# Memory values with the weights held in the array, first tiles and weights reordered over two queues, early out-projection in half portions

## The chip, the cores and the metric

The kernel runs on one core of a Trainium2 chip. TensorE multiplies matrices into PSUM, VectorE (DVE) and ScalarE (ACT) copy and compute, GpSimd (POOL) does element-wise work in SBUF, and SyncE (SP) and ScalarE have queues on which transfers are issued to the core's 16 DMA engines. The metric is the device time of one execution in microseconds; the median of the runs is compared.

## The reference

Two independent computations share a call and their outputs are joined along the last axis.

```python
# part A: a diagonal complex state space model over L = 2048 tokens, 1024 states
Bu = jnp.einsum('bld,pd->blp', x + 0j, B_bar)
for t in range(L):
    h = Lam_bar[None, :] * h + Bu[:, t, :]
y = 2.0 * jnp.einsum('blp,dp->bld', hseq, Cmat).real + x * Dskip[None, None, :]
# part B: attention in segments of 32 tokens, with 8 memory rows carried over
for s in range(n_seg):                       # 64 segments, 32 heads of 128
    h = concat([mem, x[s]], axis=1)          # 8 + 32 rows
    q, k, v = h @ Wq, h @ Wk, h @ Wv
    p = softmax(mask(q @ k.T * scale))
    o = (p @ v) @ Wo
    mem, out_s = o[:, :8], o[:, 8:]
```

(The lines of part B are shortened.) Each segment's memory is an output of the segment before it, so part B is a recurrence over 64 steps.

## The kernel before

**Part B without the recurrence.** The kernel guesses all memories first. `og` and `guess` compute, from the means of the segments, a memory row for each segment; the rows together with the given memory stand in `memT`, which is the last 73 columns (`NM`) of `xe`. `xe` holds the tokens turned (feature on the partition, token along the row). Attention then runs over all segments at once, three to a group of 96 columns, and `check` compares the guesses with what attention gave; a flag decides whether a loop with the plain recurrence (`general`) runs afterwards. In the profile it doesn't run.

**Stages.** (1) From the start to 360 us: values of the tokens (V = x Wv, one block of 4 heads at a time, 8 blocks, `v_first` and `v_pair`) are interleaved with the first half of part A (`stage1`, `post`). (2) To about 465 us: `stage2` of part A with `guess` between. (3) From 465 to 1025 us: projections of Q and K (`proj`, 18 steps for each of 16 pairs of heads), attention (`attention`, 11 units for each pair), and the values of the memory rows (`v_mem`), all interleaved by the loop in `kernel_main`: after each attention unit as many projection steps run as the count `want` says. When all projection steps are done, at unit 165 of 176, each further unit takes one piece of `early`, a part of the out-projection whose operands are ready. (4) To the end: the rest of the out-projection (`op_some`, `op`, `evac`) with `check` between.

**The order of the work.** Instructions are written in program order; a scheduler places them on each engine and may move one that is ready ahead of others. `keep_in_program_order` puts an instruction behind the one written before it on its engine. In the timeline the engines follow the written order in the loop of stage 3, while loads are issued as soon as a buffer is free.

**Around the changed places.**

- The opening: `load_rows` (L369) brings 128 tokens as rows; `turn_rows` (L372) transposes them on TensorE, 8 pieces into one PSUM tile of tag "O", and one copy (VectorE for even tiles, ScalarE for odd ones) writes them into `xe`. `v_first` (L441) turns tiles 0 to 2, then multiplies with pieces of the first Wv block for three tiles at a time, turns tile 3 before the last pieces and ends with tile 3's matmuls. The loads stand at L875 to L881: tile 0, 2 and half of the Wv pieces on SyncE's queue, tile 1, 3 and the other half on ScalarE's. Six matmuls on a cleared piece of SBUF (L887 to L891) run while the first tile is on its way.
- Memory values: `v_mem` (L497) holds 73 columns of `memT` in the array and streams 512 columns of Wv through it, 8 times; the result has memory rows on the partitions, and ScalarE copies it to SBUF, from where 7 rows go to `vx` and 66 to `vt` in DRAM. `load_v` (L580) reads both back for each pair of heads. It is called once between projection steps 9 and 10 for block 0, and at unit 4 of head pairs 0 to 6 for blocks 1 to 7.
- Early out-projection: `op_some` (L672) yields after each `op`, which is 8 matmuls; (0,0) and (1,0) with three groups of heads make six pieces.
- PSUM: tags "P", "S" and "O" with two buffers each. Projections, `v_mem` and `early` use "P", attention scores "S", attention outputs "O". A matmul into a buffer waits until its former content has been copied out.

Of the kernel before, what the change touches and what calls it, by code (L numbers as in the profile page):

```python
# [9 lines left out]
BF16 = mybir.dt.bfloat16  # L10
# [16 lines left out]
HB = 8; HP = 16  # L27
# [7 lines left out]
NMX = 7  # L35
NM = NTL + NMX
# [280 lines left out]
class PartB:  # L317
    def __init__(self, k, x, mem0, Wq, Wk, Wv, Wo, out):
        self.k = k
        self.x, self.mem0, self.out = x, mem0, out  # L320
        self.Wf = [w.rearrange("(c p) h e -> p c (h e)", p=128) for w in (Wq, Wk, Wv)]
        self.Wo = Wo.rearrange("h e d -> e h d")
        self.vx = [k.drp.tile([NSLOT, 512], BF16, name=f"b_vx{i}") for i in range(HB)]
        self.vt = [k.drp.tile([NTL, 512], BF16, name=f"b_vt{i}") for i in range(HB)]
        self.os = [k.drp.tile([T, 1024], BF16, name=f"b_os{i}") for i in range(4)]
        self.omd = k.drp.tile([MT, H * E], BF16, name="b_omd")
        self.od = k.drp.tile([128, H * L], BF16, name="f_od")
        c = k.cst
        self.m0T = c.tile([128, KC, M], BF16, name="b_m0T")
        self.gm = c.tile([128, KC, NM], FP32, name="b_gm")  # L330
        self.xbar = c.tile([128, KC, NSEG], BF16, name="b_xbar")
        self.ogT = c.tile([128, H, NSEG], BF16, name="b_ogT")
        self.accE = c.tile([128, HP * NU], FP32, name="b_accE")
        self.rall = c.tile([128, HP * NU * 4], FP32, name="b_rall")
        self.flag = c.tile([1, 1], I32, name="b_flag")
# [30 lines left out]
            if lo < hi:  # L366
                k.SP.dma_start(self.xe[:, :, lo:hi], self.x[0][lo + r:hi + r, :], transpose=True)

    def load_rows(self, t, n, xr, e):  # L369
        e.dma_start(xr[:, t:t + n, :], self.x[0][t * 128 + 64:(t + n) * 128 + 64, :].rearrange("(i p) d -> p i d", p=128))  # L370

    def turn_rows(self, t, xr):  # L372

        k = self.k
        pt = k.ps("O", (128, 1024), BF16)
        for c in range(KC):
            k.tc.keep_in_program_order(k.PE.transpose(pt[:, c * 128:(c + 1) * 128], xr[:, t, c * 128:(c + 1) * 128], k.ident[:]))
        k.copy("vs"[t % 2], self.xe[:, :, t * 128:(t + 1) * 128], pt[:].rearrange("p (c n) -> p c n", c=KC))

    def sum_x(self, q, pool):  # L380

# [59 lines left out]
    def v_first(self, w, xr, e):  # L441

        k = self.k
        for t in range(3):
            self.turn_rows(t, xr)
        p = [k.ps("A") for t in range(4)]
        for j in range(4):
            for t in range(3):
                self.v_mm(p[t], t, w, range(2 * j, 2 * j + 2))
            if j == 2:  # L450
                self.turn_rows(3, xr)
        self.v_mm(p[3], 3, w, range(KC))
        for q in range(2):
            st = self.v_tile()
            for i in range(2):
                k.copy("s", st[:, i, :], p[2 * q + i][:])
                if i == 0:
                    yield
            self.v_st(0, q, st, e)
            yield  # L460
# [34 lines left out]


    def v_mem(self, hb):  # L497
        k = self.k
        w = self.load_wv(hb)
        p = k.ps("P")  # L500
        for c in range(KC):
            k.PE.matmul(p[0:NM, :], self.memT[:, c, :], w[:, c, :], start=(c == 0), stop=(c == KC - 1))
        st = self.p3.tile([NM, 512], BF16, name="b_vmst", bufs=2)
        k.copy("s", st[:], p[0:NM, :])
        k.SP.dma_start(self.vx[hb][64:64 + NMX, :], st[0:NMX, :])
        k.SP.dma_start(self.vt[hb][:], st[NMX:NM, :])


    def qk_init(self, pool):
        V, G = self.k.V, self.k.G  # L510
        self.qk = []
        for i in range(2):
            pair = []
            for n in "qk":
                t = pool.tile([128, 2, QW], BF16, name=f"b_{n}{i}", bufs=1)
                V.memset(t[:, :, 64 + NMX:GX], 0.0)
                V.memset(t[:, :, 21 * GW + 64:21 * GW + GX], 0.0)
                V.memset(t[:, :, NG * GW:QW], 0.0)
                pair.append(t)
            self.qk.append(pair)  # L520
        self.vb, self.mb = [], []
        for i in range(2):
            t = pool.tile([GW, NG, VW], BF16, name=f"b_v{i}", bufs=1)
            G.memset(t[:, :, 0:1], 1.0)
            G.memset(t[:, :, VW - 1:VW], 1.0)
            self.vb.append(t)
        for i in range(4):
            t = pool.tile([GW, 4 * GW + 32], BF16, name=f"b_m{i}", bufs=1)
            G.memset(t[:, 4 * GW:4 * GW + 32], 0.0)
            self.mb.append(t)  # L530
# [129 lines left out]
    def wo_half(self, half, h):  # L660
        return self.wo0[h // 8][:, h % 8, :] if half == 0 else self.wo1[:, h, :]

    def op(self, t, half, q):

        k = self.k
        ol = self.ol[t // 4, q]
        tt = t % 4
        for h8 in range(8):
            h = 8 * q + h8
            k.PE.matmul(self.acc[t, half], ol[:, h8, tt * 128:(tt + 1) * 128], self.wo_half(half, h), start=(h == 0), stop=(h == H - 1))  # L670

    def op_some(self, which, qs, tag):  # L672
        o = None
        for n, (t, half) in enumerate(which):
            if tag != "O":
                self.acc[t, half] = self.k.ps(tag)[:]
            else:
                if n % 2 == 0:
                    o = self.k.ps("O")
                self.acc[t, half] = o[:, n % 2, :]  # L680
            for q in qs:
                self.op(t, half, q)
                yield

    def evac(self, t, half):
        k = self.k
# [159 lines left out]
def kernel_main(tc, A_x, A_Lre, A_Lim, A_Bre, A_Bim, A_Cre, A_Cim, A_logdt, A_Dskip, B_x, B_mem0, B_Wq, B_Wk, B_Wv, B_Wo, out,  # L846
                force=False, dbg=None):
    with ExitStack() as ctx:
# [16 lines left out]
        with pool("p1", "right") as p1:  # L865
# [6 lines left out]
            a.tab = a.wp = a.btp = b.vst = p1  # L872
            a.jf = b.rall[:, 0:TB + 1]
            xr = tmp[:, 4096:8192].rearrange("p (t d) -> p t d", t=4)
            b.load_rows(0, 1, xr, k.SP)  # L875
            b.load_rows(1, 1, xr, nc.scalar)
            b.load_rows(2, 1, xr, k.SP)
            for j in range(4):
                b.load_wv(0, wvs[0], 4, (nc.scalar, k.SP)[j % 2], [j])
            b.load_rows(3, 1, xr, nc.scalar)  # L880
            b.load_wv(1, wvs[1], 2)  # L881
            a.load_params(tmp)
            k.SP.dma_start(tmp[0:M, 0:D], b.mem0[0])
            b.load_x(512, 1024)
            b.load_x(1024, 1536)
            b.load_x(1536, T)
            wu = tmp[:, 2048:2560]  # L887
            k.V.memset(wu, 0.0)
            pw = k.ps("O")
            for i in range(6):  # L890
                k.PE.matmul(pw[:, i % 2, :], wu[:, 0:128], wu, start=True, stop=True)  # L891

            def values():
                yield from b.v_first(wvs[0], xr, k.SP)
# [84 lines left out]
        with pool("p3", "right") as p3:  # L979
            b.p3 = p3  # L980
            b.qk_init(p3)
            pr, at = b.proj(), b.attention()
            for _ in range(9):
                next(pr)
            b.v_mem(0)
            for _ in range(9):
                next(pr)
            done = 18
            b.wo0, b.acc = [], {}
            early = b.op_some([(0, 0), (1, 0)], range(3), "P")  # L990
            for n, (hp, u) in enumerate(at):
                if u == 4 and hp < 7:
                    b.v_mem(hp + 1)
                if u == 4 and 8 <= hp < 12:
                    w = k.w8((8, 512), "wo0")
                    k.SP.dma_start(w, b.Wo[:, 8 * (hp - 8):8 * (hp - 7), 0:512])
# [113 lines left out]
```

## Time and profile before

| | us |
|---|---|
| median of 3 runs | 1251.03 (1250.48 to 1251.13) |
| profiled execution | 1250.12 |
| its span in the profile | 1248.4 |
| TensorE busy | 1236.3 |
| VectorE, ScalarE, GpSimd busy | 609.4, 329.3, 199.5 |
| last matmul ends | about 1242.5 |

A line of the timeline gives start, duration, engine, source line, operation, output and inputs, and the number of instructions that were merged into it. A duration of matmuls includes the time until the last result has left the array, so what a group occupies on TensorE is the start of the next group less its own start. "PEld" is the loading of stationary operands, which overlaps the matmuls. A line of waits gives who waited for whom, the total in us, how often, and the longest. Lines are those of the kernel before.

### The profile page before, as it was taken

The numbers are of one execution on the slowest core, as the hardware profiler recorded it, in microseconds if no ns is written. First come the engines' busy times: TensorE is split into PE (matmuls) and PEld (weight loads), VectorE is DVE, ScalarE is ACT, GpSimd is POOL, SyncE is SP. The second block draws the span as 40 slices with busy tenths as digits, with TensorE's granted clock in tenths as the row PEclk, the third lists the DMA queues.
The fourth block names the chain that finished last, engine by engine and source line by source line (L and its number), as shares of the span: only waits on it lengthen the run. The fifth ranks groups of instructions, "written<-read, shape, count | busy, mean of one in ns | idle before, by whom it ended". The sixth has DMA issues, their size and how long they took to land. (4 is left out here: it accounts for less than half of the span.)

```text
span 1248.4 us, 19205 instructions
## 1 busy us (share of the span) xinstructions
PE 1236.3 (99%) x7852; PEld 651.9 (52%) x7923; DVE 609.4 (49%) x1117; ACT 329.3 (26%) x757; POOL 199.5 (16%) x284
## 2 busy tenths in 40 slices
PE   9999999999999999999999999999999999999998
PEld 4444444444455445555555655555556554454443
DVE  4889999999931122444444444444444450011000
ACT  4444434444210002323333333333233320000000
POOL 2000000000032130222222222322232230000000
PEclk9999999999999999999999999999999999999999
DMA  9932232333666557576767544645575469606000
GB/s 238 261 109 68 89 98 71 91 93 85 151 213 201 138 163 139 96 141 141 142 122 156 114 122 94 129 82 94 105 139 105 72 195 217 159 18 152 17 26 19
DMA packets 296995, 151.81 MB, mean 122 GB/s; under 512 B 138440, under 2 KB 290240, under 8 KB 296904
## 3 DMA queue, kind: packets, MB, share of 16 engines
q1 hardware_dynamic: 295640, 149.11, 51.9%
q8 instruction: 63, 1.03, 0.4%
q10 hardware_dynamic: 1264, 1.44, 0.4%
q14 instruction: 28, 0.23, 0.1%
HBM read 73.70 MB, written 43.66 MB: 94 GB/s over the span
## 5 line engine op out<-in xcount | busy, mean ns | idle before, releaser
L570 PE MATMUL psP<-b_xe,w 128*128 128x480 bf16 x2048 | 439.7, 366 | 0.0
L570 PEld LDWEIGHTS <-w 128*128 128x128 bf16 x2048 | 194.2, 98 | 185.2
L603 POOL TENSOR_TENSOR b_m<-b_e,maskB 99x396 bf16<-99x396 bf16 x160 | 139.2, 871 | 356.3 <-ACT b_e L599 356.3
L77 DVE CAST b_q<-psP 128x480 bf16<-128x480 f32 (+1 forms) x192 | 98.2, 533 | 150.9 <-PE psP L570 139.4
L411 PEld LDWEIGHTS <-b_xe 128*128 128x128 bf16 x1024 | 99.9, 98 | 120.4 <-ACT b_xe L75 0.6
L670 PEld LDWEIGHTS <-b_ol 128*128 128x128 bf16 x1024 | 99.5, 98 | 117.5
L75 ACT ACTIVATE b_k<-psP 128x480 bf16<-128x480 f32 x128 | 73.1, 571 | 314.3 <-PE psP L570 314.3
L599 ACT ACTIVATE b_e<-psS 99x396 bf16<-99x396 f32 x176 | 87.4, 496 | 173.8 <-PE psS L596 166.6
L621 DVE TENSOR_TENSOR b_ot<-psO,b_rall 99x512 bf16<-99x512 f32 x176 | 121.7, 692 | 6.4
L256 PE MATMUL psO<-w,a_bt 128*128 128x512 bf16 x496 | 114.8, 379 | 0.8
L670 PE MATMUL psS<-w,b_ol 128*128 128x512 bf16 x438 | 99.0, 379 | 0.6
L619 DVE RECIPROCAL b_rall<-psO 99x4 f32<-99x4 f32 x176 | 31.2, 177 | 136.3 <-PE psO L614 136.2
L411 PE MATMUL psS<-w,b_xe 128*128 128x512 bf16 x378 | 90.1, 379 | 0.4
L411 PE MATMUL psP<-w,b_xe 128*128 128x512 bf16 x376 | 89.8, 379 | 0.4
L256 PEld LDWEIGHTS <-a_bt 128*128 128x128 bf16 x512 | 49.7, 98 | 59.0
L310 PEld LDWEIGHTS <-a_hs 128*128 128x128 bf16 x512 | 49.5, 98 | 58.3
L614 PE MATMUL psO<-b_v,b_m 99*128 99x129 bf16 x704 | 70.5, 221 | 0.1
L77 DVE CAST b_ost<-psS 128x512 bf16<-128x512 f32 x13 | 9.0, 692 | 125.4 <-PE psS L670 112.3
L596 PEld LDWEIGHTS <-b_k 128*128 128x128 bf16 x704 | 49.8, 98 | 33.4 <-issue 0.5
L596 PE MATMUL psS<-b_q,b_k 128*128 128x99 bf16 x704 | 60.1, 208 | 0.2
L75 ACT ACTIVATE b_vst<-psS 128x512 bf16<-128x512 f32 x56 | 33.4, 597 | 98.1 <-PE psS L411 70.2
L310 PE MATMUL psS<-w,a_hs 128*128 128x512 bf16 x245 | 57.3, 380 | 0.6
(201 smaller groups left out, 1084.0 us busy)
## 6 DMA issues: line engine op xcount, KB each, us to landing
b_v<-b_vx SPq DMA_DIRECT2D x16, 1056.0 KB
b_os<-b_ot SPq DMA_DIRECT2D x16, 960.0 KB
w<-in_B_Wv_dram SPq DMA_DIRECT2D x14, 1024.0 KB
b_vx<-b_vst SPq DMA_DIRECT2D x48, 256.0 KB
w<-in_B_Wo_dram SPq DMA_DIRECT2D x12, 1024.0 KB
w<-in_B_Wq_dram SPq DMA_DIRECT2D x16, 512.0 KB
w<-in_B_Wk_dram SPq DMA_DIRECT2D x16, 512.0 KB
a_xn<-in_A_x_dram SPq DMA_DIRECT2D x32, 128.0 KB
```

The costliest lines, as they stand in the source:

```text
L75: self.S.activation(out, in_, ACT.Copy)
L77: self.V.tensor_copy(out, in_)
L256: m = PE.matmul(u[:, i, :], self.bt[:, i, c, :], self.xT[tb][:, c, :], start=(c == 0), stop=(c == KC - 1))
L310: PE.matmul(py[:], self.hs[tb][:, pc, i, tt * 128:(tt + 1) * 128], self.ct[half, i][:, pc, :], start=(pc == 0 and i == 0), stop=(pc == PC ...
L411: m = self.k.PE.matmul(p[:], self.xe[:, c, t * 128:(t + 1) * 128], w[:, c, :], start=(c == 0), stop=(c == KC - 1))
L570: PE.matmul(p[:, 0:480], w[:, i * KC + c, hh * 128:(hh + 1) * 128], self.xe[:, c, 480 * q:480 * q + 480], start=(c == 0), stop=(c == KC - 1))
L596: PE.matmul(s[:, j * GW:(j + 1) * GW], kt[:, hh, g0:g0 + 128], qt[:, hh, g0:g0 + GW], start=True, stop=True)
L599: k.S.activation(e[:], s[0:GW, 0:4 * GW], ACT.Exp, scale=float(E) ** -0.5, accum_out=self.accE[0:GW, i:i + 1])
L603: k.G.tensor_tensor(v4(m[:, 0:4 * GW]), v4(e[:]), mask[0:GW, :, :].unsqueeze(2).to_broadcast([GW, 2, 2, GW]), ALU.mult)
L614: PE.matmul(o[:, gg, cs], m[:, j * GW:j * GW + 128], vt[:, 2 * u + gg, cs], start=True, stop=True)
L621: V.tensor_tensor(ot[:, 2 * u:2 * u + 2, :].rearrange("p g (h e) -> p g h e", h=2), oa[:, :, 1:257].rearrange("p g (h e) -> p g h e", h=2) ...
L670: k.PE.matmul(self.acc[t, half], ol[:, h8, tt * 128:(tt + 1) * 128], self.wo_half(half, h), start=(h == 0), stop=(h == H - 1))
```

## The change

It has three parts.

1. `v_mem` holds 128x128 pieces of Wv in the array and streams the 73 columns of `memT` (32 matmuls for 8). The result now has the value features on the partitions; ScalarE copies 4x73 columns, a store puts them into a new DRAM tensor `vm`, a transposing load brings them back as rows (`vr`), and two stores write `vx` and `vt` as before. The function became a generator with three stops; it is started earlier (projection step 3 for block 0, unit 3 of a head pair for the others) and continued at later steps. The transfers are kept in written order. Two SBUF tiles are cleared once in `qk_init`.
2. The first tile comes in two halves, one on each queue, each followed by a piece of Wv; the other tiles and pieces alternate, and the second Wv block is spread over both queues. A turned tile takes two PSUM banks and is copied in two halves, all by VectorE; `v_first` multiplies after each turned tile what is then available. The first matmuls, now seven, read a constant of ones.
3. `op` takes a range of heads and `op_some` a number of parts; `early` is called with 2, so that it has twelve pieces of 4 matmuls.

```diff
+        self.vm = [k.drp.tile([512, 128], BF16, name=f"b_vm{i}") for i in range(HB)]
...
-    def load_rows(self, t, n, xr, e):
-        e.dma_start(xr[:, t:t + n, :], self.x[0][t * 128 + 64:(t + n) * 128 + 64, :].rearrange("(i p) d -> p i d", p=128))
+    def load_rows(self, t, xr, e, cs=slice(0, D)):
+        self.k.tc.keep_in_program_order(e.dma_start(xr[:, t, cs], self.x[0][t * 128 + 64:t * 128 + 192, cs]))
...
-        pt = k.ps("O", (128, 1024), BF16)
+        pt = k.ps("O", (128, 2, 1024), BF16)
         for c in range(KC):
-            k.tc.keep_in_program_order(k.PE.transpose(pt[:, c * 128:(c + 1) * 128], xr[:, t, c * 128:(c + 1) * 128], k.ident[:]))
-        k.copy("vs"[t % 2], self.xe[:, :, t * 128:(t + 1) * 128], pt[:].rearrange("p (c n) -> p c n", c=KC))
+            k.tc.keep_in_program_order(k.PE.transpose(pt[:, c // 4, (c % 4) * 128:(c % 4) * 128 + 128], xr[:, t, c * 128:(c + 1) * 128], k.ident[:]))
+        for i in range(2):
+            k.copy("v", self.xe[:, 4 * i:4 * i + 4, t * 128:(t + 1) * 128], pt[:, i, 0:512].rearrange("p (c n) -> p c n", c=4))
...
-        for t in range(3):
+        p = [k.ps("A") for t in range(4)]
+        for t, todo in enumerate((((0, 0, 2),), ((0, 2, 4), (1, 0, 4)), ((0, 4, 6), (1, 4, 6), (2, 0, 6)),
+                                  ((0, 6, 8), (1, 6, 8), (2, 6, 8), (3, 0, 8)))):
             self.turn_rows(t, xr)
-        p = [k.ps("A") for t in range(4)]
-        for j in range(4):
-            for t in range(3):
-                self.v_mm(p[t], t, w, range(2 * j, 2 * j + 2))
-            if j == 2:
-                self.turn_rows(3, xr)
-        self.v_mm(p[3], 3, w, range(KC))
+            for tt, c0, c1 in todo:
+                self.v_mm(p[tt], tt, w, range(c0, c1))
...
     def v_mem(self, hb):
         w = self.load_wv(hb)
         p = k.ps("P")
-        for c in range(KC):
-            k.PE.matmul(p[0:NM, :], self.memT[:, c, :], w[:, c, :], start=(c == 0), stop=(c == KC - 1))
-        st = self.p3.tile([NM, 512], BF16, name="b_vmst", bufs=2)
-        k.copy("s", st[:], p[0:NM, :])
-        k.SP.dma_start(self.vx[hb][64:64 + NMX, :], st[0:NMX, :])
-        k.SP.dma_start(self.vt[hb][:], st[NMX:NM, :])
+        for h in range(4):
+            for c in range(KC):
+                k.PE.matmul(p[:, h * NM:(h + 1) * NM], w[:, c, h * 128:(h + 1) * 128], self.memT[:, c, :],
+                            start=(c == 0), stop=(c == KC - 1))
+        st = self.vmst[hb % 2]
+        k.copy("s", st[:, :, 0:NM], p[:, 0:4 * NM].rearrange("p (h n) -> p h n", h=4))
+        pin(k.SP.dma_start(self.vm[hb].rearrange("(h p) n -> p h n", p=128), st[:]))
+        yield
+        vr = self.p3.tile([128, 512], BF16, name="b_vmr", bufs=1)
+        pin(k.SP.dma_start(vr[:], self.vm[hb][:, :], transpose=True))
+        yield
+        pin(k.SP.dma_start(self.vx[hb][64:64 + NMX, :], vr[0:NMX, :]))
+        pin(k.SP.dma_start(self.vt[hb][:], vr[NMX:NM, :]))
+        yield
...
+        self.vmst = []
+        for i in range(2):
+            t = pool.tile([128, 4, 128], BF16, name=f"b_vmst{i}", bufs=1)
+            V.memset(t[:, :, NM:128], 0.0)
+            self.vmst.append(t)
...
-    def op(self, t, half, q):
+    def op(self, t, half, q, h8s=range(8)):
...
-    def op_some(self, which, qs, tag):
+    def op_some(self, which, qs, tag, parts=1):
...
             for q in qs:
-                self.op(t, half, q)
-                yield
+                for i in range(parts):
+                    self.op(t, half, q, range(8 * i // parts, 8 * (i + 1) // parts))
+                    yield
...
-            b.load_rows(0, 1, xr, k.SP)
-            b.load_rows(1, 1, xr, nc.scalar)
-            b.load_rows(2, 1, xr, k.SP)
-            for j in range(4):
-                b.load_wv(0, wvs[0], 4, (nc.scalar, k.SP)[j % 2], [j])
-            b.load_rows(3, 1, xr, nc.scalar)
-            b.load_wv(1, wvs[1], 2)
+            q2 = (k.SP, nc.scalar)
+            for j in range(2):
+                b.load_rows(0, xr, q2[j], slice(j * 512, j * 512 + 512))
+                b.load_wv(0, wvs[0], KC, q2[j], [j])
+            for t in range(1, 4):
+                b.load_rows(t, xr, q2[t % 2])
+                b.load_wv(0, wvs[0], 4, q2[1 - t % 2], [t])
+            for j in range(2):
+                b.load_wv(1, wvs[1], 2, q2[j], [j])
...
-            wu = tmp[:, 2048:2560]
-            k.V.memset(wu, 0.0)
+            one = nc.const_aps.tensor(1.0, [128, 512], BF16)
             pw = k.ps("O")
-            for i in range(6):
-                k.PE.matmul(pw[:, i % 2, :], wu[:, 0:128], wu, start=True, stop=True)
+            for i in range(7):
+                k.PE.matmul(pw[:, i % 2, :], one[:, 0:128], one, start=True, stop=True)
...
-            for _ in range(9):
+            vm = b.v_mem(0)
+            for i in range(18):
                 next(pr)
-            b.v_mem(0)
-            for _ in range(9):
-                next(pr)
+                if i in (2, 6, 10):
+                    next(vm)
...
-            early = b.op_some([(0, 0), (1, 0)], range(3), "P")
+            early = b.op_some([(0, 0), (1, 0)], range(3), "P", 2)
             for n, (hp, u) in enumerate(at):
-                if u == 4 and hp < 7:
-                    b.v_mem(hp + 1)
+                if u == 3 and hp < 7:
+                    vm = b.v_mem(hp + 1)
+                if u in (3, 5, 7) and hp < 7:
+                    next(vm)
```

## The prediction

> **What bounds the kernel now.** I read the page's engine totals first, then the waits of TensorE, then its timeline at the three places that the change touches, then SyncE's waits.
>
> ```profile
> span 1248.4 us, 19205 instructions
> PE 1236.3 (99%) x7852; PEld 651.9 (52%) x7923; DVE 609.4 (49%) x1117; ACT 329.3 (26%) x757; POOL 199.5 (16%) x284
> ```
>
> ```profile
> PEld L377 <- DMA a_hs<-in_B_x_dram: 1.4, 1, 1.4
> PEld L614 <- POOL b_m L603: 1.1, 4, 0.3
> PEld L411 <- ACT b_xe L75: 0.6, 2, 0.3
> PEld L411 <- DVE b_xe L77: 0.4, 1, 0.4
> ```
>
> TensorE is busy for 1236.3 of 1248.4 us. Of the 12.1 left, 5.9 lie after the last matmul, about 2 ahead of the first useful work, and the waits shown are two kinds: the opening (L377, L411) and the last attention units (L614). Granted clock is full in every slice. So the time is the length of TensorE's instruction stream, and a part of the change pays only if it shortens that stream or closes one of these gaps. The chain of waits is cut off after 0.8 us on this page and says nothing here.
>
> **Price of the memory values.** In the timeline, the start of the next group minus the start of this one is what a group occupies (durations include the drain).
>
> ```profile
> 479.29 1.89 PE L502 MATMUL psP<-w,b_xe 128*73 128x512 bf16 x8
> 481.02 4.21 PE L570 MATMUL psP<-b_xe,w 128*128 128x480 bf16 x20
> ...
> 1081.26 2.32 PE L715 MATMUL psP<-c_om,w 128*128 128x73 bf16 x64
> 1083.42 7.07 PE L670 MATMUL psS<-w,b_ol 128*128 128x512 bf16 x31
> ...
> 169.41 1.10 PE L468 MATMUL psP<-b_xbar,w 128*128 128x64 bf16 x32
> 170.34 3.62 PE L256 MATMUL psO<-w,a_bt 128*128 128x512 bf16 x15
> ```
>
> Today a block of heads costs 8 matmuls that stream 512 columns of Wv: 1.73 us, 216 ns each. The new form has 32 matmuls that hold 128x128 pieces of Wv and stream 73 columns. L715 is that very shape: 64 in 2.16 us, 33.75 ns each, weight loads included. L468 holds the same Wv pieces with 64 columns: 0.93 us for 32, 29 ns each.
>
> **What the Trainium skill says.** "TensorE: Matmul & The Clock Gate", Back-to-back issue gap: a warm matmul takes N/2.4 + 2.5 ns, so 32.9 for 73 columns and 215.8 for 512; the trace agrees (33.75, 216). The same section puts a stream of load and matmul pairs with 128 columns at 81 ns; the trace doesn't agree, its pairs with 73 columns take 34. Same page, Weight-path perf modes: a 128-column weight that isn't FP32 loads fast; L715 and L468 are what that would give, while a load left exposed would show as 98 ns, the duration of a weight load here. Same page, Part 1, the HAM clock gate: the clock starts at half rate until some 3.4 us of activity; the six dummies of L891 do start 0.43 us apart, against 0.216 later. "DMA: Bandwidth & Descriptors", Issuing engines are not separate DMA queues: a second queue saves issue time, not transfer time; here the DMA engines are busy 0.9 or more of nearly every half microsecond from 2.5 to 12, so only the order of bytes can help.
>
> **Part 1, memory values.** Per block 1.73 - 32 x 0.03375 = 1.73 - 1.08 = 0.65 us off the stream; 8 blocks give **5.2 us**. Added for each block: ScalarE's copy becomes 128x292 instead of 73x512 (0.38 us for 256 columns, 0.60 for 512 in other rows, so about 0.42, shorter than today's 0.59, and hidden under projections). Then SyncE's queue gets two transfers more: a store of 128 KB (0.35 us to issue) and a transposing load of 512x128 (the 512x1024 loads take 4.0 us to issue, the 128x1024 ones 1.25, so about 0.6). That is about 1 us more of SyncE's time in each of seven 35 us periods, where it waits for some 20 us. The two memsets go to VectorE, about 0.2 us each by their size against the twelve at 465.6 us; the first projection copy needs VectorE at 466.5 and can slip by under 0.4 us behind a 1.6 us group; nothing on the path.
>
> The new wait is the chain store, transposed load, store, each in order on SyncE. Queued behind it are the loads of b_v, of projection weights and of Wv. GpSimd issues none. Who waits for those: attention of the next head pair, a period (35 us) away, except at the start.
>
> ```profile
> SPq L585 <- DMA b_vx<-b_vmst: 4.2, 1, 4.2
> ...
> 486.75 0.33 SPq L585 DMA_DIRECT2D b_v<-b_vx  x1
> ...
> 501.78 0.40 PE L614 MATMUL psO<-b_v,b_m 99*128 99x129 bf16 x4
> ```
>
> A store takes 4.2 us to land before b_v may be loaded. For block 0 the matmuls move from step 9 to step 3 of the first projection (464.7 + 3 x 1.62 = 469.6), the store is issued at about 471.3 and landed by 475.6, the turned load goes at step 7 (476) and is there by 480-481, the final stores go at step 11 (482.5 against 481.8 now), b_v is loaded from about 487.5 and lands near 491.5. It is first read at 501.8: 10 us of cover. Wv itself is asked for one unit earlier (3 instead of 4), but its loads go two blocks ahead (issued at 481.2 for the group of 542.7). If that cover were gone, each us late would be a us on the path, once. Buffers: the group after the new, shorter one needs the psum tile that was filled just before it. That tile's copy starts 0.20 us after its last matmul and takes 0.57 or 0.66, so it is free after 0.9; the new group covers 1.08 of that (1.73 before). Cost nothing, but the margin is 0.2.
>
> **Part 2, early out-projection.** Six fillers of 8 matmuls now run with units 165 to 170; then the attention units stand alone and TensorE waits for GpSimd's masks (0.87 us a unit against 0.42 us of its own work).
>
> ```profile
> 1019.53 0.40 PE L614 MATMUL psO<-b_v,b_m 99*128 99x129 bf16 x4
> 1020.02 0.82 PE L596 MATMUL psS<-b_q,b_k 128*128 128x99 bf16 x8
> 1020.97 0.41 PE L614 MATMUL psO<-b_v,b_m 99*128 99x129 bf16 x4
> 1021.22 0.34 PE L596 MATMUL psS<-b_q,b_k 128*128 128x99 bf16 x4
> 1021.59 0.38 PE L670 MATMUL psS<-w,b_ol 128*128 128x512 bf16 x1
> ```
>
> With 0.178 us for a front (four of L596), 0.238 for a back (four of L614) and 0.216 for a filler, the gaps are 0.25, 0.59, 0.19 here and 0.22 at 1022.27: **1.25 us**. Twelve fillers of four fit the 13 units to the end: 0.42 + 0.86 = 1.28 us a unit, above GpSimd's 0.87, VectorE's 0.87 and ScalarE's 0.70. The way from a front to its mask is about 2.1 us (496.25 front, 496.69 exponential, 497.36 mask, 0.87 long); the back of a unit comes 2.4 to 2.7 us after its front. So all 1.25 is won. Bound from below: 0.4, if the order written isn't the order scheduled.
>
> **Part 3, the opening.**
>
> ```profile
> 1.33 2.74 PE L891 MATMUL psO<-a_hs 128*128 128x512 bf16 x6 [1.33 <-DVE a_hs L888]
> 4.54 1.51 PE L377 MATMUL psO<-ident,a_hs 128*128 128x128 bf16 x16 [0.46 <-DMA a_hs<-in_B_x_dram]
> 6.35 0.61 PE L377 MATMUL psO<-ident,a_hs 128*128 128x128 bf16 x8 [0.30 <-DVE b_xe L77]
> ...
> 14.25 1.89 PE L411 MATMUL psS<-a_hs,b_xe 128*128 128x512 bf16 x8
> ```
>
> From 4.54 to 14.25 are 9.7 us for 32 transposes (0.056 us) and 32 matmuls (0.216) of 8.7. Tile 0 alone, halved over both queues, is 256 KB instead of the 512 KB of tiles 0 and 1 that arrive together at 4.54; by the bytes moved in each half microsecond (0.25 MB by 3.2 us, 0.6 us to completion as now) it is there at about 3.9. The seven dummies need no memset, start near 0.9 and end near 3.9. But tile 1 now comes behind 256 KB of Wv: 1.05 MB have moved at about 5.35, so it is there near 5.9, and until then only 8 transposes and 2 matmuls can run. From 5.9 there are 24 transposes and 30 matmuls, 7.8 us, plus some 0.2 of waits for the half copies, all on VectorE now (0.69 us a tile before; two halves about 0.43 each by the same rate, 3.4 us in all, under 8 us of TensorE). ScalarE's queue issues six transfers instead of four, at 0.45 us, and is free at 3.5, ahead of its table load and long before its first copy of values (12.35). SyncE's queue keeps six, so what follows on it (parameters, transposed tokens) goes when it did; the second Wv block, in two halves on both queues, is needed near 13.9, and 3.1 MB have moved by 10.7. End at 13.9: **0.4 us** won. Bounds: +1.0 if tile 1 lands by 5.3, -0.5 if the gap keeps the clock low for longer. Neither is shown by the trace of before; I take the middle of the working.
>
> **Sum.** 5.2 + 1.25 + 0.4 = 6.85. The profiled execution took 1250.12, so 1243.3; it lies 0.9 below the median of the runs shown, 1251.03, from which the same step gives **1244.2**.
>
> **Rivals.**
> (a) One small part fails: the spread is rescheduled or the opening gets worse. 6.85 - 0.85 to 6.85 - 2.1: 1245.0 to 1246.3. For it: both gains come from arguments on order. Against: the timeline follows the written order there now.
> (b) A wait takes the place of the shorter group: 0.65 us a block, from the 0.2 us psum margin or a late chain, and only the 1.65 of the other parts stays: 1249.4. Against: copies start 0.20 us after their matmuls throughout.
> (c) Slower: the stationary loads of Wv are exposed at L502's new place. It decides from 54 ns a matmul (1.73/32); at 98 it is 3.14 us a block, +1.41 x 8 - 1.65 = +9.6: 1260.7. For it: the 98 ns weight load, and the skill's 81. Against: L468 did the same on the same tiles at 29.
>
> **How the numbers follow.** Forecast 0.76, (a) 0.14, (b) 0.05, (c) 0.05. The forecast's own spread is 1242.8 to 1245.4 (opening +0.6/-0.9, spread -0.4, runs 0.65 apart); with (a) the range is 1242.4 to 1246.6. A difference under 0.2%, 2.5 us, can't be told from none in this kernel: faster 0.90, same 0.05, slower 0.05.
>
> **What would show it.** L502's groups: 32 of 128x73, 1.08 us to the next group, eight times; no wait of L570 behind them. From unit 165 on, fillers of four between every front and back, no wait of L614 on L603. First transposes near 3.9, second Wv block's first matmul near 13.9. Wrong if TensorE shows a wait on b_v, on psP or on w between 465 and 1020, or if the new group takes over 1.7 us.

## The result, and the profile after

| | before | changed |
|---|---|---|
| median, us | 1250.76 (1250.13 to 1251.13) | 1245.97 (1245.06 to 1247.67) |
| profiled execution, us | 1250.12 | 1245.06 |
| its span, us | 1248.4 | 1243.3 |

The ratio is 0.9964, 95% interval 0.9947 to 0.9981: 4.8 us faster, where 6.85 had been worked out. (A fourth run of the kernel before moved its median from 1251.03 to 1250.76.) The page of the changed kernel, the lines that answer to those of before:

```profile
span 1243.3 us, 19697 instructions
PE 1234.8 (99%) x8116; PEld 653.3 (53%) x8116; DVE 611.2 (49%) x1124; ACT 326.3 (26%) x755; POOL 199.7 (16%) x284
```

TensorE still sets the time: 1234.8 of 1243.3 us. It is busy for only 1.5 us less than before although the span is 5.1 us shorter, mainly because some records of before are missing (7852 matmuls beside 7923 weight loads, where after has 8116 of each); so the parts are better read from where groups start than from busy sums. Its waits (us in total, times, longest):

```profile
PEld L378 <- DMA a_hs<-in_B_x_dram: 2.4, 2, 2.0
PEld L907 <- issue: 2.2, 6, 0.8
PEld L413 <- DVE b_xe L77: 1.4, 2, 0.8
```

The wait for GpSimd's masks in the attention units (1.1 us before) is gone. The wait for rows of tokens has grown from 1.4 to 2.4 us, the wait for copies of turned tokens from 1.0 (0.6 for ScalarE's, 0.4 for VectorE's) to 1.4. Both are in the opening. Each stage, from the start of one named group to the start of another:

| stretch | before | changed | difference |
|---|---|---|---|
| start to the second Wv block's first matmul | 14.25 | 15.58 | **+1.33** |
| from there to the first projection of stage 3 | 450.46 | 450.46 | 0 |
| from there to the first early filler | 541.79 | 536.62 | **-5.17** |
| last attention units, with the fillers | 16.27 | 15.00 | **-1.27** |
| from there to the last group's start | | | +0.2 |

In the fourth row 9 matmuls that the changed kernel runs later are counted at 0.216 us each, so that both hold the same work. The sum, -4.9, is the shift of the last group (1235.41 to 1230.53).

The timeline of TensorE in the changed kernel, first at the start of stage 3, then at the last attention units:

```profile
466.04 5.02 PE L584 MATMUL psP<-b_xe,w 128*128 128x480 bf16 x24
470.90 1.24 PE L504 MATMUL psP<-b_xe,w 128*128 128x73 bf16 x32
471.99 21.22 PE L584 MATMUL psP<-b_xe,w 128*128 128x480 bf16 x104
...
1014.18 1.03 PE L684 MATMUL psP<-w,b_ol 128*128 128x512 bf16 x4
1015.04 0.34 PE L610 MATMUL psS<-b_q,b_k 128*128 128x99 bf16 x4
1015.22 0.40 PE L628 MATMUL psO<-b_v,b_m 99*128 99x129 bf16 x4
1015.46 1.03 PE L684 MATMUL psP<-w,b_ol 128*128 128x512 bf16 x4
...
1017.43 0.40 PE L628 MATMUL psO<-b_v,b_m 99*128 99x129 bf16 x4
1017.66 10.52 PE L684 MATMUL psS<-w,b_ol 128*128 128x512 bf16 x48
```

The new group of memory values occupies 471.99 - 470.90 = 1.09 us, with no wait after it. The fillers are now four matmuls long and stand between every front and back. The opening:

```profile
0.86 3.15 PE L907 MATMUL psO<-const-bfloat16-1.0 128*128 128x512 bf16 x7 [0.86 <-PEq L1109]
3.79 1.06 PE L378 MATMUL psO<-ident,a_hs 128*128 128x128 bf16 x8
5.37 0.74 PE L413 MATMUL psS<-a_hs,b_xe 128*128 128x512 bf16 x2 [0.52 <-DVE b_xe L77]
7.49 0.62 PE L378 MATMUL psO<-ident,a_hs 128*128 128x128 bf16 x8 [1.38 <-DMA a_hs<-in_B_x_dram]
7.95 0.59 PE L413 MATMUL psS<-a_hs,b_xe 128*128 128x512 bf16 x2
...
15.58 1.89 PE L413 MATMUL psS<-a_hs,b_xe 128*128 128x512 bf16 x8
```

Tile 0 is turned from 3.79 on, 0.75 us earlier than before, as was wanted. Then TensorE stands for 1.38 us, until 7.49, because tile 1 isn't there.

### The profile page after: what moved, and what is told of

Read it like the earlier page. It is cut to its first block, busy times and chain, and to the rows that moved or that the text cites. A ratio compares the mean times of both kernels' runs of the same rounds, so it can differ in the third digit from the quotient of the medians.

```text
span 1243.3 us, 19697 instructions
## 1 busy us (share of the span) xinstructions
PE 1234.8 (99%) x8116; PEld 653.3 (53%) x8116; DVE 611.2 (49%) x1124; ACT 326.3 (26%) x755; POOL 199.7 (16%) x284
## 4 chain that ended last, share of the span: by engine, by line
PE 99%; DMA 0%; ACTq 0%; DVE 0%; ACT 0%; issue 0%
PE psP L584 33%; PE psS L684 10%; PE psP L413 9%; PE psO L256 9%; PE psS L413 9%; PE psP L684 6%; PE psP L310 4%; PE psS L310 4%; PE psP L567 4%; PE psO L628 3%; PE psS L610 3%; PE psO L684 2%; PE psP L504 1%; PE psP L730 1%; PE psO L481 1%; DMA a_hs<-in_B_x_dram 0%
```

## The experiments

Theory 1: the three parts add up; memory values and spread give what was worked out (together 6.45 us), and the new opening loses time, because tile 1 comes too late. Its rivals: the loss isn't the opening's but is spread over the other parts (a wait behind L504, a late chain of memory values), or the opening as such gains and the runs merely scatter. What in the opening is to blame was then asked in two further groups: the new order of work or the new loads; the order of the bytes, the number of transfers, or the short rows of the half tiles (each row of a half tile is 1 KB; this last is called theory R).

All results, each against the kernel before on the same chip:

| kernel | median, us | ratio (95% interval) | second Wv block starts, us | extra at half clock, us |
|---|---|---|---|---|
| changed | 1245.97 | 0.9964 (0.9947 to 0.9981) | 15.58 | 0.5 |
| e1: change with the old opening | 1243.99 | 0.9948 (0.9935 to 0.9962) | 13.93 | 0 |
| e2: the new opening alone | 1252.79 | 1.0017 (1.0010 to 1.0023) | 17.57 | 2.1 |
| e3: memory values alone | 1244.73 | 0.9958 (0.9944 to 0.9971) | 13.88 | 0.2 |
| e4: spread alone | 1249.38 | 0.9991 (0.9984 to 0.9997) | 14.02 | 0 |
| e5: new loads, old order of work | 1248.87 | 0.9985 (0.9977 to 0.9994) | 18.15 | 1.5 |
| e6: old loads, new order of work | 1244.82 | 0.9957 (0.9940 to 0.9973) | 14.89 | 0.1 |
| e7: tile 1 ahead of the Wv pieces | 1246.29 | 0.9964 (0.9953 to 0.9976) | 15.54 | 0.4 |
| e8: same byte order, 256 KB each | 1243.79 | 0.9947 (0.9931 to 0.9964) | 14.23 | 0.5 |
| e9: only tile 0 in halves | 1244.17 | 0.9954 (0.9937 to 0.9970) | 14.99 | 0.9 |
| e10: only the first Wv quarter in halves | 1246.16 | 0.9968 (0.9956 to 0.9981) | 16.04 | 1.3 |
| e11: halves with full rows | 1246.79 | 0.9975 (0.9964 to 0.9985) | 15.62 | 0 |
| e12: old opening with the new dummies | 1243.95 | 0.9946 (0.9930 to 0.9963) | 16.00 | 2.5 |

e1 to e4 were made beside a kernel before of 1250.48 us, e5 to e8 beside 1250.59, e9 to e12 beside 1250.39. The last two columns come from the one profiled execution of each, which in e5 and e11 was 1.4 to 1.7 us faster than the median and in e12 1.9 slower. The last column is an estimate from the timelines: at full pace the transposes start 0.056 us apart and the matmuls of 512 columns 0.216, at half pace 0.107 and 0.427; what the starts lie further apart than at full pace, from the first transpose to the second Wv block, is added up. Before has 0.4 us there, so the 1.33 us between before and the change are not the clock's. Where a wait follows at once, such time can be hidden.

### The parts alone (e1 to e4)

**e1** is the change without part 3: the loads, `turn_rows`, `v_first` and dummies of before.

```diff
-            for j in range(2):
-                b.load_rows(0, xr, q2[j], slice(j * 512, j * 512 + 512))
-                b.load_wv(0, wvs[0], KC, q2[j], [j])
...
+            b.load_rows(0, 1, xr, k.SP)
+            b.load_rows(1, 1, xr, nc.scalar)
+            b.load_rows(2, 1, xr, k.SP)
+            for j in range(4):
+                b.load_wv(0, wvs[0], 4, (nc.scalar, k.SP)[j % 2], [j])
+            b.load_rows(3, 1, xr, nc.scalar)
+            b.load_wv(1, wvs[1], 2)
```

> The changed kernel with the opening of before (loads, turned tiles, first matmuls, dummies); memory values and spread as changed. Theory 1 (the parts add up, the new opening lost 1.3 us): the second Wv block's first matmul is back at 14.25 us and the time is 1250.8 - 5.2 - 1.25 = 1244.3, about 1.3 below the changed kernel. Rival 2 (the opening gave its 0.4 in most executions and the profiled one was an exception; memory values or spread brought less than forecast outside the profile): 1246 or more.

Measured: 1243.99 us (1243.61 to 1244.29), 6.49 less than before; 6.45 had been worked out for these two parts. Its timeline has the second Wv block early:

```profile
13.93 1.89 PE L412 MATMUL psS<-a_hs,b_xe 128*128 128x512 bf16 x8
```

**e2** is the kernel before with part 3 alone, that is with the edits of `load_rows`, `turn_rows`, `v_first`, the load order and the dummies.

```diff
-            b.load_rows(0, 1, xr, k.SP)
-            b.load_rows(1, 1, xr, nc.scalar)
...
+            for j in range(2):
+                b.load_rows(0, xr, q2[j], slice(j * 512, j * 512 + 512))
+                b.load_wv(0, wvs[0], KC, q2[j], [j])
...
+            for i in range(7):
+                k.PE.matmul(pw[:, i % 2, :], one[:, 0:128], one, start=True, stop=True)
```

> The kernel before with the new opening alone. Theory 1: second Wv block's first matmul near 15.6 instead of 14.25, time 1.3 us above the kernel before (1252.1), with more spread between runs than before. Rival 2: 0.4 below (1250.4).

Measured: 1252.79 us (1250.72 to 1254.88), 2.3 more than before, with an interval that lies wholly above 1. TensorE's timeline of e2:

```profile
7.86 0.62 PE L377 MATMUL psO<-ident,a_hs 128*128 128x128 bf16 x8 [1.82 <-DMA a_hs<-in_B_x_dram]
8.36 0.59 PE L412 MATMUL psS<-a_hs,b_xe 128*128 128x512 bf16 x2
8.99 1.89 PE L412 MATMUL psP<-a_hs,b_xe 128*128 128x512 bf16 x4
10.67 1.06 PE L377 MATMUL psO<-ident,a_hs 128*128 128x128 bf16 x8
...
17.57 0.59 PE L412 MATMUL psS<-a_hs,b_xe 128*128 128x512 bf16 x2
```

and by stretches (columns: stretch, its length, TensorE's busy time and instructions, granted clock, DMA share, GB/s):

```profile
7.80:9.00 1.20, 1.10 (x11) 0.98 1.02 352
9.00:10.00 1.00, 1.00 (x3) 0.50 1.06 384
```

After an idle time of 1.82 us the four matmuls from 8.99 on start 0.42 us apart, eight transposes take 0.86 us instead of 0.45: the clock is at half until 12.38. That costs 0.82 + 0.41 + 0.42 = 1.65 us on top of the wait. It accounts for the difference to the changed kernel in this column (17.57 against 15.58): 1.65, and 0.37 for the later tile 1. So the 2.3 us are in part the wait and in part the clock. The other executions of e2 fit that: the three whose mean granted clock (the recorded share of TensorE's full clock) was 1.000 took 1250.72 to 1251.74 us, the five with 0.997 or less 1253.18 to 1254.88. The changed kernel had a gap of 1.38 us in its profiled execution and no half clock after it.

**e3** has part 1 alone, **e4** part 2 alone, each on the kernel before.

```diff
 e3, v_mem
-            k.PE.matmul(p[0:NM, :], self.memT[:, c, :], w[:, c, :], start=(c == 0), stop=(c == KC - 1))
+                k.PE.matmul(p[:, h * NM:(h + 1) * NM], w[:, c, h * 128:(h + 1) * 128], self.memT[:, c, :],
+                            start=(c == 0), stop=(c == KC - 1))
...
 e4
-            early = b.op_some([(0, 0), (1, 0)], range(3), "P")
+            early = b.op_some([(0, 0), (1, 0)], range(3), "P", 2)
```

> The kernel before with the new memory values alone, begun and continued at the new steps. Theory 1: 8 x 0.65 = 5.2 us less (1245.6), no wait of TensorE between 465 and 1005 us. Rival 2: 4 us less or under.

> The kernel before with the early out-projection in twelve pieces alone. Theory 1: 1.25 us less (1249.5), the waits of L614's line on GpSimd gone. Rival 2: 0 to 0.4 less.

Measured: e3 1244.73 us (1244.17 to 1246.39), 5.75 less than before (5.2 worked out); e4 1249.38 us (1248.54 to 1250.13), 1.10 less (1.25 worked out), and TensorE's waits for GpSimd's masks are gone from its list. Parts 1 and 2 deliver, alone and together. What is missing from the sum is the opening's. Theory 1 stands; the rivals that look for the loss behind L504 or in scatter fall with e1 and e2.

### Loads or work, order or size (e5 to e8)

**e5** keeps the new loads and takes back `turn_rows` and `v_first`; **e6** keeps the new work and dummies and takes back the loads.

```diff
 e5, v_first
+        for t in range(3):
             self.turn_rows(t, xr)
-            for tt, c0, c1 in todo:
-                self.v_mm(p[tt], tt, w, range(c0, c1))
...
 e6
-                b.load_rows(0, xr, q2[j], slice(j * 512, j * 512 + 512))
-                b.load_wv(0, wvs[0], KC, q2[j], [j])
...
+            b.load_rows(0, xr, k.SP)
+            b.load_rows(1, xr, nc.scalar)
+            b.load_rows(2, xr, k.SP)
```

> The changed kernel with the transposes, copies and order of matmuls of before; loads and dummies as changed. Theory L (the loads are the cause: tile 1 comes late): transposes of tile 1 again near 7.5 us, second Wv block's first matmul at 15 or later, time at least 1 us above the kernel with the old opening (1244.0). Theory C (the new order of matmuls and the half copies on VectorE are the cause): as the old opening, 14 and 1244.0 to 1244.5.

> The changed kernel with the loads in the old sizes and order; new dummies, half copies and order of matmuls. Theory L: tile 1 is there with tile 0 near 4.5, second Wv block's first matmul at 14.0 to 14.3, time 1244.0 to 1244.4. Theory C: 15 or later, about 1246.

Measured: e5 1248.87 us (1246.79 to 1249.72), e6 1244.82 us (1244.14 to 1245.83). The timelines of e5 and of e6:

```profile
7.91 1.04 PE L378 MATMUL psO<-ident,a_hs 128*128 128x128 bf16 x8 [3.17 <-DMA a_hs<-in_B_x_dram]
...
18.15 1.03 PE L412 MATMUL psS<-a_hs,b_xe 128*128 128x512 bf16 x4
```

```profile
6.39 0.59 PE L413 MATMUL psS<-a_hs,b_xe 128*128 128x512 bf16 x2 [1.10 <-DMA a_hs<-in_B_Wv_dram]
...
14.89 1.89 PE L413 MATMUL psS<-a_hs,b_xe 128*128 128x512 bf16 x8
```

With the new loads and the old work TensorE stands for 3.17 us, and the kernel loses 4.9 us to e1 by the medians; in the profiled execution it is 4.2, about 1.5 of them at half clock, most of it after that gap. With the old loads and the new work it loses 0.8: no wait for tile 1, but 1.10 us for Wv, which the old loads bring later. (Theory L had put the second block of e6 at 14.0 to 14.3; that missed.) So the loads do the damage, and the new order of work softens it: it has something to multiply while tile 1 is on its way.

**e7** puts tile 1 ahead of the Wv pieces, in halves of 128 KB too. **e8** keeps the change's order of bytes, but tile 0 and the first quarter of Wv are one transfer of 256 KB each, not two of 128 KB.

```diff
 e7
+            for j in range(2):
+                b.load_rows(1, xr, q2[j], slice(j * 512, j * 512 + 512))
+            for j in range(2):
                 b.load_wv(0, wvs[0], KC, q2[j], [j])
...
 e8
-            for j in range(2):
-                b.load_rows(0, xr, q2[j], slice(j * 512, j * 512 + 512))
-                b.load_wv(0, wvs[0], KC, q2[j], [j])
-            for t in range(1, 4):
+            for t in range(4):
```

> The changed kernel with tile 1, in halves on both queues, ahead of all Wv pieces. Theory L1 (tile 1 is late because 256 KB of Wv are ahead of it in the queues): tile 1's transposes near 5.0, second Wv block at 14.0 or earlier, time 1244.3 or less. Theory L2 (small transfers of 128 KB at the head of both queues slow the engines down): tile 1 still after 6 us, second Wv block after 14.8.

> The changed kernel with the same order of bytes in whole transfers of 256 KB: tile 0 on one queue, the first quarter of Wv on the other, then as changed. Theory L1: tile 0 near 4.5, tile 1 as late as in the change, 7 us or more, second Wv block after 15. Theory L2: tile 1 at 5.9 as the bytes say, second Wv block at 14.3 or earlier.

Measured: e7 1246.29 us (1244.21 to 1247.26): TensorE now waits 1.88 us for Wv in place of tile 1, and the second block starts at 15.54, as in the change; theory L1, the order, had put it at 14.0 or earlier and falls. e8 1243.79 us (1243.20 to 1244.53). The timelines of e7 and of e8:

```profile
6.73 0.59 PE L413 MATMUL psS<-a_hs,b_xe 128*128 128x512 bf16 x2 [1.88 <-DMA a_hs<-in_B_Wv_dram]
```

```profile
3.92 1.03 PE L378 MATMUL psO<-ident,a_hs 128*128 128x128 bf16 x8
5.48 0.79 PE L413 MATMUL psS<-a_hs,b_xe 128*128 128x512 bf16 x2 [0.52 <-DVE b_xe L77]
6.14 0.62 PE L378 MATMUL psO<-ident,a_hs 128*128 128x128 bf16 x8
...
14.23 1.89 PE L413 MATMUL psS<-a_hs,b_xe 128*128 128x512 bf16 x8
```

Tile 0 is turned only 0.13 us later than in the change, and tile 1 at 6.14 without a wait for it: that bears out L2's forecast of 5.9. Changing the order moves the wait from the tile to the weights; whole transfers, larger and fewer, take it away. Size and number change together here and can't be told apart. The transfer view of the first 5 us shows what the wait goes with (40 slices of 0.125 us, what the DMA engines moved), for before, the change and e8:

```profile
GB/s 0 0 0 0 0 0 0 0 0 0 0 0 0 0 49 82 82 131 33 33 311 344 344 344 410 213 197 246 410 361 426 443 394 402 401 401 369 377 336 344
```

```profile
GB/s 0 0 0 0 0 0 0 0 0 0 0 0 0 0 33 147 147 172 123 213 270 352 377 385 369 361 311 262 246 221 180 147 147 148 221 238 197 180 172 188
```

```profile
GB/s 0 0 0 0 0 0 0 0 0 0 0 0 0 0 66 131 98 131 131 229 279 311 352 262 238 229 221 254 295 311 287 311 353 377 393 410 401 393 418 385
```

From 3.5 us on (the last twelve figures) before moves 389 GB/s in the mean, e8 361, the change 190. Summed up, the change has even moved more than before until 3.5 us (0.44 MB against 0.35); it falls back after that, as its first small transfers end. 1.05 MB had moved at about 5.35 us in before and in e8, at 6.15 in the change. These are single executions, but others with the same loads agree: from 3.5 to 5 us e2 and e5, with the change's loads, move 224 and 179 GB/s; e1, e3, e4, e6 and e12, with the loads of before, 305 to 380.

### Which of the small transfers (e9 to e12)

**e9** halves tile 0 alone, **e10** the first quarter of Wv alone, **e11** cuts tile 0 into two halves of 64 tokens with full rows of 2 KB. **e12** is e1 with the seven dummies on a constant in place of the six with a memset, to see whether they matter.

```diff
 e9
-                b.load_wv(0, wvs[0], KC, q2[j], [j])
+            b.load_wv(0, wvs[0], 4, q2[0], [0])
...
 e10
+            b.load_rows(0, xr, q2[0])
             for j in range(2):
-                b.load_rows(0, xr, q2[j], slice(j * 512, j * 512 + 512))
-                b.load_wv(0, wvs[0], KC, q2[j], [j])
+                b.load_wv(0, wvs[0], KC, q2[1], [j])
...
 e11
-                b.load_rows(0, xr, q2[j], slice(j * 512, j * 512 + 512))
+                tc.keep_in_program_order(q2[j].dma_start(xr[64 * j:64 * j + 64, 0, :], b.x[0][64 + 64 * j:128 + 64 * j, :]))
...
 e12, against e1
-            for i in range(6):
-                k.PE.matmul(pw[:, i % 2, :], wu[:, 0:128], wu, start=True, stop=True)
+            for i in range(7):
+                k.PE.matmul(pw[:, i % 2, :], one[:, 0:128], one, start=True, stop=True)
```

> The changed kernel, only tile 0 in halves of 512 columns on both queues; the first quarter of Wv whole (256 KB). Theory S (each small transfer at the head costs rate when it ends, whatever it carries): tile 1 is turned between the whole form (6.1 us) and the change (7.5), near 6.8; second Wv block near 14.9. Theory R (the 1 KB pieces of the token rows are the slow ones): as the change, 7.5 and 15.6.

> The changed kernel, tile 0 whole on one queue (256 KB), the first quarter of Wv in two transfers of 128 KB on the other. Theory S: as the kernel with only tile 0 in halves, near 6.8 and 14.9. Theory R: as the whole form, 6.1 and 14.2.

> The changed kernel, tile 0 in halves of 64 tokens with full rows of 2 KB, all else as changed. Theory S: as the change, tile 1 near 7.5, second Wv block near 15.6, time 1246. Theory R: as the whole form, 6.1 and 14.2, time 1243.8.

> The opening of before, but the seven matmuls on the constant instead of six on a cleared tile; memory values and spread as changed. They start at 0.86 instead of 1.33 us. If the earlier start lifts the clock earlier, the first 16 transposes take 1.0 us or less and the second Wv block starts near 13.6, time 1243.7; if not, 14.0 and 1244.0 as the old opening.

Measured: e9 1244.17 us (1243.94 to 1246.08), e10 1246.16 (1245.82 to 1247.55), e11 1246.79 (1245.13 to 1248.03), e12 1243.95 (1243.41 to 1245.86). The timelines of e10, of e11 and of e12:

```profile
4.69 1.03 PE L378 MATMUL psO<-ident,a_hs 128*128 128x128 bf16 x8 [0.69 <-DMA a_hs<-in_B_x_dram]
...
7.37 1.04 PE L378 MATMUL psO<-ident,a_hs 128*128 128x128 bf16 x8
8.20 1.06 PE L413 MATMUL psS<-a_hs,b_xe 128*128 128x512 bf16 x2
...
16.04 1.89 PE L413 MATMUL psS<-a_hs,b_xe 128*128 128x512 bf16 x8
```

```profile
6.50 0.59 PE L413 MATMUL psS<-a_hs,b_xe 128*128 128x512 bf16 x2 [1.55 <-DMA a_hs<-in_B_Wv_dram]
```

```profile
4.69 2.83 PE L378 MATMUL psO<-ident,a_hs 128*128 128x128 bf16 x24 [0.69 <-DMA a_hs<-in_B_x_dram]
...
16.00 1.89 PE L412 MATMUL psS<-a_hs,b_xe 128*128 128x512 bf16 x8
```

Theory R falls: with full rows (e11) the rate from 3.5 to 5 us is 137 GB/s, lower still, and Wv comes late (waits of 1.55 and 0.71 us). Theory S, that each small transfer costs the same, falls too: it put tile 1 near 6.8 us in both e9 and e10, and it was turned at 6.26 and at 7.37. With tile 0 alone in halves (e9) the rate is 306, which the loads of before reach too (305 to 389), the waits for Wv are 0.60 and 0.55 us, and 0.4 us is lost to e8, no more than the scatter of these runs. With only the Wv quarter in halves (e10) 370 GB/s flow from 3.5 on, but 147 from 2 to 3.5; tile 0, whole and on one queue, is there only at 4.69, and 2.4 us are lost by the medians. In the profiled execution e10 is 1.8 us behind e8: 0.8 for the later tile 0, and about 0.8 because the half clock lasted until about 9 us. So neither kind of halves alone brings the fall after 3.5 us that both together bring in the change, which loses 2.2.

e12's median is that of e1, so the dummies cost nothing as a rule. But in the execution that was profiled (1245.86 us) the 24 transposes took 0.11 us each where e1's took 0.056: after a gap of 0.69 us the clock stayed at half until about 10 us.

## Why the prediction was right, and where it was wrong

The change is faster and the time lies in the stated range; the size was 4.8 us, not 6.85. What happened is rival (a) in its form "the opening gets worse", with 1245.0 to 1246.3 worked out, and not the forecast proper: 1245.97 lies outside the forecast's own spread (to 1245.4), and inside the stated range only because that took in (a), which had been given 0.14. Two of the three parts were right by their mechanism; that the third didn't carry the sum out of the range is owed to that allowance.

**Part 1, 5.2 us: right.** Eight groups of 8 matmuls became eight of 32; the stretch that holds them is 5.17 us shorter, and L504 occupies 1.08 to 1.09 us as reckoned from L715's 33.75 ns. Rival (c), exposed weight loads, is excluded with that (it decided at 1.73 us a group). So, for this case, is the 81 ns that the Trainium skill ("TensorE: Matmul & The Clock Gate", Back-to-back issue gap) gives for a pair of load and matmul with 128 columns: 34 ns were measured with 73 columns, and the transposes, with 128 columns and a load each, start 56 ns apart. Rival (b) is excluded too: between 466 and 1020 us no wait of TensorE on b_v, on w or on the psum tile behind L504 appears. The margin of 0.2 us held. What the turn saves can be counted: 8 x 512 = 4096 columns are streamed for a block before, 32 x 73 = 2336 after.

The chain of memory values went by the steps given, but not by their times. SyncE's issues for block 0:

```profile
472.65 1.10 SPq L508 DMA_DIRECT2D b_vm<-b_vmst  x1
...
479.97 1.19 SPq L511 DMA_TRANSPOSE b_vmr<-b_vm  x1
482.50 0.31 SPq L513 DMA_DIRECT2D b_vx<-b_vmr  x1
482.88 0.30 SPq L514 DMA_DIRECT2D b_vt<-b_vmr  x1
483.84 0.33 SPq L599 DMA_DIRECT2D b_v<-b_vx  x1
```

The transposing load takes 1.19 us to issue, where "about 0.6" had been put by size between two rows, and the store 1.10 instead of 0.35. b_v, on the other hand, is loaded from 483.84, not "from about 487.5": the store into b_vx had landed within 1.4 us, where 4.2 had been carried over from before. SyncE waits 18.8 us in all for the store to land and 13.9 for the turned rows. All of that was hidden, as said.

**Part 2, 1.25 us: right.** 1.27 by the stretch, 1.10 by e4's median. The order written was the order run.

**Part 3, +0.4 us: wrong in sign.** It cost 1.33 us in the change's profiled execution, 2.0 by the medians of the change and e1, and 2.3 alone (e2). Together with the 0.4 that was expected, 1.33 makes 1.73, which is about what the profiled execution missed its forecast by (1245.06 against 1243.3). The step that failed is "1.05 MB have moved at about 5.35, so tile 1 is there near 5.9". The bytes were counted rightly and the 5.35 fits the kernel before. But the rate was that of before's transfers of 256 KB, applied to another set of transfers: in the change the same bytes need until 6.15. That is half of the 1.6 us by which tile 1 is late, turned at 7.49. The other half is not the rate's: with the forecast's own 0.6 us to completion, the last bytes of tile 1 moved near 6.9, and by 7.0 us 1.37 MB had moved. By this estimate some 0.3 MB that were queued behind tile 1 went ahead of its last bytes. The sentence "so only the order of bytes can help" left out that the sizes of the transfers change too. e8, with the same order in transfers of 256 KB, has tile 1 at 6.14 and is 2.2 us faster than the change. The bound of -0.5 for this part was too narrow for the same reason: it allowed for a low clock, but not for late bytes, and the two came together in e2, where the half clock after the gap cost 1.65 us. Of the other steps of Part 3 these held: dummies from 0.86 on, tile 0 at 3.79 (3.9), and the two half copies of a tile, 0.76 us of VectorE where 0.86 was reckoned. These did not, and cost nothing: ScalarE's queue was free at 5.6 us, not 3.5, and what follows on SyncE's queue did not go when it did before (parameters from 7.46 instead of 6.14, transposed tokens from 10.47 instead of 9.04). The 3.1 MB had moved in before at 11.0 us, not at 10.7.

**Left open.** Why the split slows the loads is not shown. The fall stands where the first small transfers end. The engines weren't short of issued bytes: at 3.5 us the change had issued 1.5 MB and moved 0.44. Nor is it merely a pause between transfers: by the time that their packets took, the engines were busy from 3.5 to 5 us for 0.76 of the time in the change and 0.79 in e5, but for all of it (1.05) in e2, which has the same loads. Whether the share-out over the 16 engines got worse, no run tells. Nor is it settled what drops the clock and what lifts it. Gaps of 3.17 us (e5) and 1.82 (e2) were followed by half clock, gaps of 1.88 (e7), 1.55 (e11) and 1.38 (the change) were not, so the length of a gap alone doesn't decide; and full pace was reached by 4.64 us in e1, but only near 10 in e12. That the change's own runs lie 2.6 us apart, before's 1.0, would follow from it. e2's granted clocks speak for that; the change's, 0.999 for its two faster runs and 0.998 for its two slower ones, are too coarse to show it.

**Better versions.** e1, e8 and e12 end at 1243.8 to 1244.0 us by their medians, 6.4 to 6.8 under the kernels before beside them; so parts 1 and 2 with the old opening, or with the new one in whole transfers, are about 2 us better than the change. The intervals of their ratios still overlap with the change's, but every run of e1 and e8 (up to 1244.53) is faster than every run of the change (from 1245.06), and e2 shows the change's opening alone to be slower than that of before.

## What to carry to other kernels

A forecast of when bytes arrive has to take its rate from transfers of the same size and number; the bytes moved per half microsecond belong to the transfers that moved them. To have a first tile sooner, reorder whole transfers before splitting them: here the split won 0.13 us for tile 0 and lost 1.35 for tile 1. And a matmul group with few rows in the array (here 73) is worth turning round where that streams fewer columns and the loads of the other operand stay hidden under the matmuls, as they did here; the price was read from another group of the same shape in the same profile, and held to 1%.

## What the runs showed of the hardware that was not expected

- Splitting 512 KB at the head of two queues into four transfers of 128 KB lowered the rate from 3.5 to 5 us from 361 (e8) to 190 GB/s; in e2 and e5, with the same split, it was 224 and 179.
- In these openings a queue issued four transfers at once and the fifth after a pause: in the change SyncE's at 3.46 and ScalarE's at 3.62 us, although the fourth issue was over at 2.7.

```profile
2.21 0.47 SPq L371 DMA_DIRECT2D a_hs<-in_B_x_dram  x1
3.46 1.89 SPq L405 DMA_DIRECT2D a_hs<-in_B_Wv_dram  x2
```

- An idle TensorE of 1.82 us early in the kernel was followed by some 3.4 us at half clock (e2), and one of 3.17 us likewise (e5); one of 1.88 us was not (e7).
- How soon the clock first rose differed by more than 5 us between executions: e1's transposes ran at full pace from 4.64 us, e12's matmuls were still 0.43 us apart after 9. The recorded granted clock doesn't show this: it reads 1.00 for e12 from 8 to 9 us.
- Issue times on one queue vary by a factor of three with the shape of the transfer: the store of `v_mem` into 512 rows of 128 took 1.10 us, those of 7 and of 66 rows of 512 took 0.31 and 0.30.
